# Second transform: the last three block products of a column group accumulated in one pair of banks, two column groups alternating

## The chip, the core and the metric

The kernel runs on one core of a Trainium2 chip. The metric is the device time of one execution in microseconds (us); the median of three runs before the change is 1871.7 us (1870.88 to 1874.08).

Five instruction queues work side by side: TensorE (PE; its weight loads are shown apart as PEld), VectorE (DVE), ScalarE (ACT), GpSimd (POOL) and SyncE (SP), which here issues almost all transfers. Matrix products end in eight accumulator banks of 128 x 512 fp32 (PSUM), from which VectorE or ScalarE takes them away.

## The reference

Four layers follow each other on a 2048 x 512 activation, each added to its input: Fourier mixing, segmented attention with a memory, Fourier mixing again, attention again. The change is in the third layer.

```
def _A_ref(x, dft_seq_re, dft_seq_im, dft_hid_re, dft_hid_im):
    a = jnp.einsum("bsd,ed->bse", x, dft_hid_re)
    b = jnp.einsum("bsd,ed->bse", x, dft_hid_im)
    y = jnp.einsum("ts,bse->bte", dft_seq_re, a) - jnp.einsum("ts,bse->bte", dft_seq_im, b)
    return y
...
x = x + _A_ref(_layernorm(x, axis=-1), A_dft_seq_re, A_dft_seq_im, A_dft_hid_re, A_dft_hid_im)
x = x + _B_ref(_layernorm(x, axis=-1), B_wq, B_wk, B_wv, B_wo, B_beta)
x = x + _A_ref(_layernorm(x, axis=-1), A_dft_seq_re, A_dft_seq_im, A_dft_hid_re, A_dft_hid_im)
x = x + _B_ref(_layernorm(x, axis=-1), B_wq, B_wk, B_wv, B_wo, B_beta)
```

## The kernel before

**The transforms.** The kernel swaps the two matrix products of the mixing: first over the sequence (cosine and sine matrix, 2048 x 2048 each), then over the hidden dimension. The 2048 result columns are handled in four column groups of 512 (`tcn` 0 to 3). Every fp32 operand is split into a high and a low part (`split`, lines 97 to 107: ScalarE writes the high part, VectorE the low one), and `matmul3` (lines 109 to 112) takes high x high, high x low and low x high, so that one 128 x 128 by 128 x 512 product is three matmuls.

**First and second transform.** The first (`direct`, `contract`) multiplies plainly. As it goes, it writes sums and differences of the matrix blocks to scratch memory (`sums`, line 301), and the second transform uses them in a seven-product scheme for a 2 x 2 block product in place of eight. A product (`P1` to `P7`) runs over eight steps `k`; a step is one right-hand block `t` of 128 x 512, and two left-hand column blocks `m` = 0, 1, each with its own bank and three matmuls: six matmuls a step. The left-hand sides come from `left`: normalised rows `xa` (P1, P7, P2, P4), and combinations of rows made by `add_rows`, `xb` (P6 and P5) and `xs` (P3).

**Order of the products.** `PHASES` sets it. In the first four phases two products run interleaved, step by step, for two column groups in turn. In the last phase P6, P5 and P3 run interleaved, for each of the four column groups: 24 steps a group, 96 in all, in six banks at a time. `bank` (line 117) hands out the eight banks in rotation, so a product's first matmul waits until the earlier user of that bank has been taken away.

**Taking away.** When a product is done, `product` (lines 349 to 358) adds it to or subtracts it from each block `c[tcn, j]` that has it as a term, as `TERMS` lists: in the last phase P6 goes into three blocks, P5 into two and P3 into one, each in two halves `m`. That is 12 VectorE instructions `c<-c,m` (line 358) for a column group. `c` then is read by `split_u` (tiles `us`), and by the hidden-dimension products `y` (`hidden`, `hidden_last`).

**Right-hand blocks.** `read_block` (line 258) has SP read the raw block into a ring of eight (`cring`), from the given matrix (`in_ct`) for P1, P2 and P3 and from the sums (`sum`) for the others, and then splits it into a tile `chi` or `clo`. Despite the names, each such tile holds a high and a low part; the two names alternate, with three buffers each, so that six blocks may be ready at a time.

**Order of the work.** `place` puts generators at numbered slots, and the loop at line 1058 runs through the slots. A step of a product is one slot; a block is read ten slots and split four slots ahead of it. PE keeps that order. On the other engines a scheduler may move an instruction that is ready earlier.

Of the kernel before, what the change touches and what calls it, by code (L numbers as in the profile page):

```python
# [14 lines left out]
ALU = mybir.AluOpType  # L15
# [24 lines left out]
HALF = NT // 2  # L40
# [4 lines left out]
    "P7": (((1, 1), (0, 1), ALU.add),),  # L45
    "P2": (((0, 0), (0, 1), ALU.add),),
    "P4": (((1, 0), (1, 1), ALU.add),),
    "P6": tuple((j, j, ALU.subtract) for j in ((0, 1), (1, 0), (1, 1))),
    "P5": tuple((j, j, ALU.add) for j in ((0, 1), (1, 1))),
    "P3": (((0, 1), (0, 1), ALU.add),),  # L50
}
PHASES = (
    (("P1", "P7"), (0, 1)),
    (("P2", "P4"), (0, 1)),
    (("P1", "P7"), (2, 3)),
    (("P2", "P4"), (2, 3)),
    (("P6", "P5", "P3"), range(4)),
)


# [1 line left out]
def spectral_infini_kernel(  # L62
# [13 lines left out]
    V, A, G, T = nc.vector, nc.scalar, nc.gpsimd, nc.tensor  # L76
# [6 lines left out]
    def in_order(engine, name):  # L83
        op = getattr(engine, name)

        def call(*args, **kwargs):
            return tc.keep_in_program_order(op(*args, **kwargs))  # L87

        return call

    T = SimpleNamespace(matmul=in_order(T, "matmul"), transpose=in_order(T, "transpose"))
# [5 lines left out]
    def split(hi, lo, src, scale=1.0, lo_engine=V, hi_engine=None):  # L97
        if hi_engine is V:
            return V.tensor_copy(hi, src), V.tensor_tensor(out=lo, in0=src, in1=hi.bitcast(F32), op=ALU.subtract)  # L99
        else:  # L100
            pin(A.activation(hi, src, AF.Copy, scale=scale))  # L101
        if scale == 1.0:
            lo_engine.tensor_tensor(out=lo, in0=src, in1=hi.bitcast(F32), op=ALU.subtract)  # L103
        else:
            V.scalar_tensor_tensor(
                lo, src, scale, hi.bitcast(F32), op0=ALU.mult, op1=ALU.subtract
            )

    def matmul3(ps, lhsT, rhs, first, last):
        T.matmul(ps, lhsT(0), rhs(0), start=first, stop=False)  # L110
        T.matmul(ps, lhsT(0), rhs(1), start=False, stop=False)
        T.matmul(ps, lhsT(1), rhs(0), start=False, stop=last)

    def rows(ap, i):
        return ap[i * P : (i + 1) * P, :]
# [1 line left out]
    def bank(name, shape=(P, 512), dtype=F32):  # L117
        return psum.tile(list(shape), dtype, name=name, tag="bank", bufs=8)

    def pair(name, tag, bufs, dtype=F32R):  # L120
        return sb.tile([P, 2, 512], dtype, name=name, tag=tag, bufs=bufs)

    def load_rows(src, name="xt"):
        t = sb.tile([P, 512], F32, name=name, tag="xt", bufs=4)
        nc.sync.dma_start(t, src)
        return t
# [32 lines left out]
    def normal(xt, mv, rr):  # L159
        xn = sb.tile([P, D], F32, name="xn", bufs=2)  # L160
        V.tensor_scalar(xn, xt, mv[:, 0:1], rr, op0=ALU.subtract, op1=ALU.mult)
        return xn
# [16 lines left out]
    def place(order, gen, *at):  # L179
        for t in itertools.chain(*at):  # L180
            slots.setdefault(t, []).append((order, gen))

    def run_from(t, n, step=1):
        return range(t, t + n * step, step)
# [7 lines left out]
    def place_spectral(x_in, x_out, t0, end, ln_at, direct):  # L192
        xa, xb, xs, us, wdt, c, right = ({} for _ in range(7))
        start = t0
# [25 lines left out]
        def add_rows(k):  # L220
            xt = [load_rows(x_in[i]) for i in (k, k + HALF)]
            yield
            e, o = (
                normal(xt[n], row_mv[:, i], row_r[:, i : i + 1])
                for n, i in enumerate((k, k + HALF))
            )
            a, b = slice(0, D // 2), slice(D // 2, D)
            V.tensor_tensor(out=e[:, b], in0=o[:, b], in1=e[:, b], op=ALU.subtract)
            V.tensor_tensor(out=e[:, a], in0=e[:, a], in1=e[:, b], op=ALU.add)
            V.tensor_tensor(out=o[:, a], in0=e[:, a], in1=o[:, a], op=ALU.subtract)  # L230
            xb[k] = pair("xb", "w", 16)
            split(xb[k][:, 0], xb[k][:, 1], e)
            if k % 2 == 0:
                xs[k // 2] = pair("xs", "w", 16)
            half = xs[k // 2][:, :, k % 2 * 256 : (k % 2 + 1) * 256]
            split(half[:, 0], half[:, 1], o[:, a])
            yield

        def left(name, k, h, m):
            src, col = {  # L240
                "P1": (xa.get(k), 0),
                "P7": (xa.get(k), 2),
                "P2": (xa.get(k + HALF), 0),
                "P4": (xa.get(k + HALF), 2),
                "P6": (xb.get(k), 0),
                "P5": (xb.get(k), 2),
                "P3": (xs.get(k // 2), k % 2 * 2),
            }[name]
            return src[:, h, (col + m) * P : (col + m + 1) * P]

        def new_right(src):
            tag = ("chi", "clo")[count[0] % 2]
            count[0] += 1
            t = pair(tag, tag, 3)
            split(t[:, 0], t[:, 1], src)
            return t

        def read_block(tcn, name, k):
            if not ring:
                ring.append(sb.tile([P, 2 * LT, 512], F32, name="cring", tag="xT", bufs=1))  # L260
            raw = ring[0][:, blocks_read[0] % (2 * LT)]
            blocks_read[0] += 1
            j = SOURCE[name]
            if isinstance(j, tuple):
                nc.sync.dma_start(raw, ct[j[0], tcn, k, :, j[1]])
            else:
                nc.sync.dma_start(raw, sums[tcn, k][j])
            yield
            right[tcn, name, k] = new_right(raw)
            yield  # L270
# [64 lines left out]
        def product(tcn, name):  # L335
# [22 lines left out]
                        V.tensor_tensor(out=dst, in0=c[tcn, base][:, m], in1=ps[m], op=op)  # L358
            yield

        def split_u(tcn, tt):
            sl = slice(tt * P, (tt + 1) * P)
            for cc in range(2):
                home = ("ut", 8) if (tcn, cc) == (TC - 1, 1) else ("w", 16)
                us[tcn, tt, cc] = t = pair("us", *home)
                for half in range(2):
                    hi, lo = (
                        t[:, h, half * 256 : (half + 1) * 256].rearrange("p (m s) -> p m s", s=P)
                        for h in range(2)
                    )  # L370
                    split(hi, lo, c[tcn, (half, cc)][:, :, sl])
            yield
# [45 lines left out]
        if direct:  # L418
            for tcn in range(TC):
                t = start + 8 * HALF * tcn  # L420
                place(2, contract(tcn), run_from(t, 4 * HALF, 2))
                for k in range(HALF):
                    place(3, read_pairs(tcn, k), [t + 8 * k - 12, t + 8 * k - 4, t + 8 * k + 3])
        else:
            t = start
            for names, tcns in PHASES:
                for tcn in tcns:
                    for n, name in enumerate(names):
                        at = run_from(t + n, HALF, len(names))
                        place(2, product(tcn, name), at)  # L430
                    for k in range(HALF):
                        for n, name in enumerate(names):
                            u = t + k * len(names) + n
                            place(3, read_block(tcn, name, k), [u - 10, u - 4])
                    t += HALF * len(names)
            u = t - 4 * 3 * HALF
            for k in range(HALF):
                place(3, add_rows(k), [u - 48 + 6 * k, u - 44 + 6 * k])
        for k in range(2 * DT):
            cc, d = k // DT, k % DT  # L440
            tag = "craw" if k < 2 else ("chi", "clo")[k % 2]
            t = end - 7 + k if k < 2 else end - 3 + (k - 2) // 2
            place(3.5, load_split(wdt, (cc, d), wd[cc, d], "wdt", tag, 2 if k < 2 else 3), [t - 5, t])
        nh = 2 * DT * LT
        for tcn in range(TC):
            if tcn == 0:
                at = [end + k // 2 for k in range(nh)]
            elif tcn < TC - 1:
                at = [end + nh // 2 + ((tcn - 1) * nh + k) // 3 for k in range(nh)]
            else:  # L450
                at = run_from(end + nh // 2 + 2 * nh // 3 + 1, 2 * DT, 2)
            for tt in range(LT):
                place(3.7, split_u(tcn, tt), [at[tt * 2 * DT if tcn < TC - 1 else 0] - 4])
            place(4, (hidden if tcn < TC - 1 else hidden_last)(tcn), at)
# [554 lines left out]
    def w_at(b):  # L1009
        return lambda k: b - 52 + 2 * k if k < 12 else b - 14 + 2 * (k - 12)  # L1010

    place_spectral(
        x_tiles, mids[0], a1, b1 - LEAD,
        [((0,), a1 - 36), ((HALF,), a1 - 2)] + [((k, k + HALF), a1 - 6 + 8 * k) for k in range(1, HALF)],
        True,
    )
    place_attention(mids[0], mids[1], b1, w_at(b1), lambda k: b1 + LB + 8 + k // 2)
    place_spectral(
        mids[1], mids[2], a2, b2 - LEAD,
        [((2 * j, 2 * j + 1), a2 + t) for j, t in enumerate((-40, -24, -8, 2, 14, 20, 32, 38))],  # L1020
# [83 lines left out]
```

## Time and profile before

| | |
|---|---|
| median of three runs | 1871.7 us (1870.88 to 1874.08) |
| profiled execution, time | 1868.32 us |
| profiled execution, span | 1866.6 us |
| mean granted TensorE clock | 0.989 |
| busy: PE / DVE / ACT / POOL | 95% / 70% / 57% / 28% |
| second transform: products with `xa` from, with `xb` and `xs` from, `y` from | 934.1 / 1134.4 / 1271.2 us |

The span is from the first to the last profiled instruction; 1.72 us of the profiled execution's time lie outside it. A row of a timeline gives the start, the length, the engine, the line, the tiles (written<-read), and the number of instructions that follow each other; in brackets stands how long the engine was idle before it and whose end released it. Matmuls overlap in the pipeline, so what counts is the distance between starts, not the length.

### The profile page before, as it was taken

Reading aid. Unit: us, or ns where it says so; the run is one execution under the profiler, and the core shown is the slowest. Engines: PE = TensorE matmul, PEld = TensorE weight load, DVE = VectorE, ACT = ScalarE, POOL = GpSimd, SP = SyncE. Lnnn points to the kernel's source line nnn. Section 1 sums busy time; section 2 is a strip of 40 time slices with the busy share of each in tenths; the row PEclk is TensorE's granted clock in tenths of the full one; section 3 lists DMA queues with packets and bytes.
Section 4 is the critical chain, followed back from the end, with each engine's and each line's share of the span. In section 5 each row is a group of like instructions: output and inputs, shape, how many; then the busy total and the mean of one; then the engine's idle time right before and its main releaser. Section 6 shows DMA issues by size and latency. Waiting matters only on the chain. (4 is left out here: it accounts for less than half of the span.)

```text
span 1866.6 us, 32022 instructions
## 1 busy us (share of the span) xinstructions
PE 1781.6 (95%) x10336; PEld 1291.0 (69%) x10336; DVE 1315.2 (70%) x4073; ACT 1056.1 (57%) x2292; POOL 526.1 (28%) x831
## 2 busy tenths in 40 slices
PE   7999999999889999999899999999988999999998
PEld 6788888888556666665468888778865566666555
DVE  7854544663787887877967686768557778787684
ACT  3222221432678787778864455444427877777785
POOL 4400000003345354445542000000124444444442
PEclk9999999999999999999999999999998999999999
DMA  6766556453534443435357687654544334344331
GB/s 214 225 217 214 189 181 210 161 170 127 177 125 134 131 134 104 147 119 181 106 170 231 196 259 215 180 170 141 172 144 142 121 113 150 120 132 136 121 122 51
DMA packets 165656, 296.50 MB, mean 159 GB/s; under 512 B 17776, under 2 KB 66928, under 8 KB 165488
## 3 DMA queue, kind: packets, MB, share of 16 engines
q1 hardware_dynamic: 162224, 293.68, 49.9%
q8 instruction: 81, 1.33, 0.3%
q10 hardware_dynamic: 3264, 0.79, 0.2%
q14 instruction: 87, 0.71, 0.1%
HBM read 192.95 MB, written 100.66 MB: 157 GB/s over the span
## 5 line engine op out<-in xcount | busy, mean ns | idle before, releaser
L605 DVE CUSTOM_DVE_ANT_0 junk<-nat,mask 128x512 bf16<-128x512 f32 (+3 forms) x1024 | 496.3, 485 | 196.6 <-PE nat L87 162.2
L671 ACT ACTIVATE pT<-sT 128x512 f32<-128x512 f32 x640 | 371.5, 599 | 13.5 <-ACT sT L670 1.7
L674 POOL TENSOR_SCALAR_AFFINE_SELECT pT<-pT 128x256 f32<-128x256 f32 (+1 forms) x448 | 198.6, 457 | 451.8 <-ACT pT L671 388.1
L87 PE MATMUL u<-chi,xa 128*128 128x512 f32 x1024 | 317.3, 391 | 7.3 <-DVE xa L99 7.3
L87 PE MATMUL sT<-stkq,stkk 99*128 99x256 bf16 (+3 forms) x1024 | 249.1, 306 | 10.1 <-DMA stkq<-mt 4.6
L87 PE MATMUL nat<-stkk,stkq 96*128 96x512 bf16 (+3 forms) x1024 | 247.0, 303 | 7.1 <-DVE mx L605 2.7
L670 ACT ACTIVATE sT<-sT 128x256 f32<-128x256 f32 (+1 forms) x640 | 207.3, 335 | 53.0 <-PE sT L87 48.3
L87 PEld LDWEIGHTS u<-chi,xa 128*128 128x128 f32 x1024 | 193.5, 189 | 47.2 <-ACT chi L101 7.3
L144 POOL TENSOR_TENSOR r<-ve,half_neg 128x2 f32<-128x2 f32 (+1 forms) x33 | 22.7, 688 | 665.2 <-DVE ve L142 660.1
L87 PE MATMUL u<-clo,xa 128*128 128x512 f32 x512 | 201.5, 394 | 2.4 <-DVE clo L103 2.0
L87 PE MATMUL y<-wdt,us 128*128 128x512 f32 x768 | 181.9, 390 | 0.0
L87 PEld LDWEIGHTS <-stkk 99*128 99x128 bf16 x1024 | 82.2, 99 | 136.7 <-issue 122.9
L87 PEld LDWEIGHTS y<-wdt,us 128*128 128x128 f32 x768 | 143.6, 188 | 29.7
L87 PE MATMUL pv_bank<-pT,vt 128*17 128x512 f32 (+3 forms) x2048 | 151.2, 435 | 0.0
L87 PEld LDWEIGHTS <-stkq 96*128 96x128 bf16 x1024 | 94.6, 99 | 62.4 <-issue 22.8
L87 PE MATMUL pvv<-wv,xT 128*128 128x512 f32 x384 | 129.8, 451 | 3.7 <-DVE mx L605 3.7
L87 PE MATMUL pqk<-xT,wq 128*128 128x512 f32 x384 | 130.3, 448 | 0.0
L87 PE MATMUL po<-wo,oh 128*128 128x512 f32 x384 | 122.3, 433 | 4.2 <-DVE mx L605 2.2
L87 PE MATMUL pqk<-xT,wk 128*128 128x512 f32 x384 | 124.7, 433 | 0.0
L87 PEld LDWEIGHTS u<-clo,xa 128*128 128x128 f32 x512 | 96.6, 189 | 26.6 <-DVE clo L103 6.7
L87 PEld LDWEIGHTS pv_bank<-pT,vt 128*17 128x17 f32 x2048 | 53.6, 97 | 85.9 <-issue 82.7
L101 ACT ACTIVATE chi<-cring 128x512 fp32r<-128x512 f32 x112 | 70.6, 630 | 69.3 <-DVE clo L103 35.0
(138 smaller groups left out, 3038.3 us busy)
## 6 DMA issues: line engine op xcount, KB each, us to landing
sum<-sring SPq DMA_DIRECT2D x32, 1024.0 KB
cring<-sum SPq DMA_DIRECT2D x128, 256.0 KB
stkq<-scrq SPq DMA_DIRECT2D x64, 384.0 KB
stkk<-scrk SPq DMA_DIRECT2D x64, 384.0 KB
cring<-in_ct SPq DMA_DIRECT2D x96, 256.0 KB
sring<-in_ct SPq DMA_DIRECT2D x32, 512.0 KB
xt<-mid SPq DMA_DIRECT2D x64, 256.0 KB
craw<-in_ct SPq DMA_DIRECT2D x30, 512.0 KB
```

The costliest lines, as they stand in the source:

```text
L87: return tc.keep_in_program_order(op(*args, **kwargs))
L101: pin(A.activation(hi, src, AF.Copy, scale=scale))
L144: G.tensor_tensor(out=r, in0=ve, in1=half_neg[:, :n], op=ALU.pow)
L605: V.tensor_tensor_reduce(junk[:, :n], src, mask[:, 512 - n :], 1.0, 3e38, ALU.add, ALU.min, dst,)
L670: A.activation(blocks, blocks, AF.Relu)
L671: A.activation(dst, ps, AF.Exp, scale=-SCALE)
L674: G.affine_select(blocks, blocks, pattern=[[0, n] for n in blocks.shape[1:-1]] + [[1, P]], compare_op=ALU.is_ge, fill=0.0, base=0, channel ...
```

## The change

In the last phase the three products are no longer kept apart. `product` no longer handles P6, P5 and P3; a new function `chained` opens two banks for a column group, runs the eight steps of P6 in them, adds the two banks to `c[tcn, (1, 0)]`, goes on in the same two banks with P5 without clearing them, adds P6 + P5 to `c[tcn, (1, 1)]`, goes on with P3 and adds P6 + P5 + P3 to `c[tcn, (0, 1)]`. That is six instructions `c<-c,m` for a column group in place of 12. For the sums to come out with one sign, `add_rows` makes two of its three combinations with the opposite sign, with `scalar_tensor_tensor` in place of `tensor_tensor`.

Two column groups alternate: eight steps of P6 for group 0, eight of P6 for group 1, then P5 for group 0, P5 for group 1, P3 for 0, P3 for 1; then the same for groups 2 and 3. The number of steps (96), of matmuls and of blocks read stays as it was; the reading order of the blocks follows the new order of the steps. `add_rows` stays at the same slots: its last call ends two slots ahead of the phase.

```
 CHAIN = {"P6": (1, 0), "P5": (1, 1), "P3": (0, 1)}
...
+            V.scalar_tensor_tensor(e[:, a], e[:, a], -1.0, e[:, b], op0=ALU.mult, op1=ALU.subtract)
+            V.scalar_tensor_tensor(o[:, a], e[:, a], -1.0, o[:, a], op0=ALU.mult, op1=ALU.subtract)
...
+        def chained(tcn):
+            ps = [bank(f"m{m}") for m in range(2)]
+            for name, j in CHAIN.items():
+                for k in range(HALF):
+                    t = right[tcn, name, k]
+                    for m in range(2):
+                        matmul3(
+                            ps[m],
+                            lambda h: left(name, k, h, m),
+                            lambda h: t[:, h],
+                            (name, k) == ("P6", 0),
+                            k == HALF - 1,
+                            skip_group_check=True,
+                        )
+                    if k < HALF - 1:
+                        yield
+                for m in range(2):
+                    dst = c[tcn, j][:, m]
+                    V.tensor_tensor(out=dst, in0=dst, in1=ps[m], op=ALU.add)
+                yield
...
+            u = t
+            for tcns in (0, 1), (2, 3):
+                at = {tcn: [] for tcn in tcns}
+                for name, tcn in itertools.product(CHAIN, tcns):
+                    at[tcn] += run_from(t, HALF)
+                    for k in range(HALF):
+                        place(3, read_block(tcn, name, k), [t + k - 10, t + k - 4])
+                    t += HALF
+                for tcn in tcns:
+                    place(2, chained(tcn), at[tcn])
             for k in range(HALF):
                 place(3, add_rows(k), [u - 48 + 6 * k, u - 44 + 6 * k])
```

On PE, the place where one pair of banks follows another. Before, at the end of column group 1's 24 steps and the start of group 2's (`m0` and `m1` are the two banks of a product, the numbers tell the products apart, `chi` and `clo` are right-hand blocks):

```order
L87 MATMUL m0_12676<-chi_12856,xb_12388 128x512 x3
L87 MATMUL m1_12677<-chi_12856,xb_12388 128x512 x3
L87 MATMUL m0_12688<-clo_12866,xs_12311 128x512 x3
L87 MATMUL m1_12689<-clo_12866,xs_12311 128x512 x3
L87 MATMUL m0_12922<-chi_12876,xb_11829 128x512 x3
L87 MATMUL m1_12923<-chi_12876,xb_11829 128x512 x3
L87 MATMUL m0_12934<-clo_12892,xb_11829 128x512 x3
L87 MATMUL m1_12935<-clo_12892,xb_11829 128x512 x3
L87 MATMUL m0_12946<-chi_12906,xs_11832 128x512 x3
L87 MATMUL m1_12947<-chi_12906,xs_11832 128x512 x3
```

After the change, on PE, the end of group 1's P6 and the start of group 0's P5 (banks 12406 and 12407, which group 0's P6 filled eight steps earlier):

```order
L84 MATMUL m0_12490<-chi_12518,xb_12308 128x512 x3
L84 MATMUL m1_12491<-chi_12518,xb_12308 128x512 x3
L84 MATMUL m0_12490<-clo_12528,xb_12388 128x512 x3
L84 MATMUL m1_12491<-clo_12528,xb_12388 128x512 x3
L84 MATMUL m0_12406<-chi_12538,xb_11829 128x512 x3
L84 MATMUL m1_12407<-chi_12538,xb_11829 128x512 x3
L84 MATMUL m0_12406<-clo_12548,xb_11906 128x512 x3
L84 MATMUL m1_12407<-clo_12548,xb_11906 128x512 x3
```

Where six new banks were wanted within three steps, two wanted again are those of eight steps ago.

On VectorE, the taking away of column group 0 among the splits of right-hand blocks (`cring` is the raw ring). Before, its 12 instructions stand among six splits (behind the 26th to the 32nd of the phase); the first of them:

```order
L103 TENSOR_TENSOR clo_12634<-cring_10387,clo_12634 128x512
L358 TENSOR_TENSOR c_10870<-c_10870,m0_12406 128x512
L358 TENSOR_TENSOR c_11417<-c_11417,m0_12406 128x512
L358 TENSOR_TENSOR c_10906<-c_10906,m0_12406 128x512
L103 TENSOR_TENSOR chi_12648<-cring_10387,chi_12648 128x512
L358 TENSOR_TENSOR c_10870<-c_10870,m1_12407 128x512
L358 TENSOR_TENSOR c_11417<-c_11417,m1_12407 128x512
L358 TENSOR_TENSOR c_10906<-c_10906,m1_12407 128x512
L358 TENSOR_TENSOR c_10870<-c_10870,m0_12418 128x512
L103 TENSOR_TENSOR clo_12660<-cring_10387,clo_12660 128x512
L358 TENSOR_TENSOR c_10906<-c_10906,m0_12418 128x512
```

After the change, the taking away of group 0's P6:

```order
L100 TENSOR_TENSOR clo_12486<-cring_10387,clo_12486 128x512
L376 TENSOR_TENSOR c_11417<-c_11417,m0_12406 128x512
L100 TENSOR_TENSOR chi_12498<-cring_10387,chi_12498 128x512
L376 TENSOR_TENSOR c_11417<-c_11417,m1_12407 128x512
L100 TENSOR_TENSOR clo_12508<-cring_10387,clo_12508 128x512
L100 TENSOR_TENSOR chi_12518<-cring_10387,chi_12518 128x512
L100 TENSOR_TENSOR clo_12528<-cring_10387,clo_12528 128x512
L100 TENSOR_TENSOR chi_12538<-cring_10387,chi_12538 128x512
```

Two instructions stand alone there, behind the splits of steps 12 and 13 of the phase, and such a pair comes again every eight splits (behind 12 and 13, 20 and 21, and so on to 92 and 93; the last pair behind all 96). Outside this phase the queues keep their order, but for a few neighbours that change places on VectorE, SP and GpSimd in the stretch of the `y` products and in the attention behind it; ScalarE's order is the same throughout.

More of the change, by code (lines that the diff above doesn't have):

```diff
@@ L47 @@
     "P4": (((1, 0), (1, 1), ALU.add),),
-    "P6": tuple((j, j, ALU.subtract) for j in ((0, 1), (1, 0), (1, 1))),
-    "P5": tuple((j, j, ALU.add) for j in ((0, 1), (1, 1))),
-    "P3": (((0, 1), (0, 1), ALU.add),),
 }
+CHAIN = {"P6": (1, 0), "P5": (1, 1), "P3": (0, 1)}
 PHASES = (
@@ L56 @@
     (("P2", "P4"), (2, 3)),
-    (("P6", "P5", "P3"), range(4)),
 )
@@ L107, in split, with matmul3 @@
             )
[L109 to L112, printed above, removed]
+    def matmul3(ps, lhsT, rhs, first, last, **kw):
+        T.matmul(ps, lhsT(0), rhs(0), start=first, stop=False, **kw)
+        T.matmul(ps, lhsT(0), rhs(1), start=False, stop=False, **kw)
+        T.matmul(ps, lhsT(1), rhs(0), start=False, stop=last, **kw)
     def rows(ap, i):
@@ L228, in add_rows @@
             V.tensor_tensor(out=e[:, b], in0=o[:, b], in1=e[:, b], op=ALU.subtract)
-            V.tensor_tensor(out=e[:, a], in0=e[:, a], in1=e[:, b], op=ALU.add)
-            V.tensor_tensor(out=o[:, a], in0=e[:, a], in1=o[:, a], op=ALU.subtract)
+            V.scalar_tensor_tensor(e[:, a], e[:, a], -1.0, e[:, b], op0=ALU.mult, op1=ALU.subtract)
+            V.scalar_tensor_tensor(o[:, a], e[:, a], -1.0, o[:, a], op0=ALU.mult, op1=ALU.subtract)
             xb[k] = pair("xb", "w", 16)
@@ L435, in place_spectral @@
                     t += HALF * len(names)
-            u = t - 4 * 3 * HALF
+            u = t
[8 more added lines that the diff above has]
+                    place(2, chained(tcn), at[tcn])
             for k in range(HALF):
```

## The prediction

> **What bounds the kernel now.** I read the page first, then busy times by stretch, then the waits and the timeline of the stretch that the change touches.
>
> ```profile
> span 1866.6 us, 32022 instructions
> PE 1781.6 (95%) x10336; PEld 1291.0 (69%) x10336; DVE 1315.2 (70%) x4073; ACT 1056.1 (57%) x2292; POOL 526.1 (28%) x831
> ...
> 1134.36:1271.15 136.79, 132.24 (x578) 107.64 (x576) 91.86 (x145) 62.87 (x102) 0.00 (x0) 1.00 0.60 171
> 1134.36:1168.36 34.00, 34.00 (x152) 28.15 (x151) 20.95 (x33) 15.81 (x25) 0.00 (x0) 1.00 0.65 185
> 1168.36:1173.13 4.77, 3.25 (x13) 2.09 (x12) 4.77 (x9) 1.27 (x2) 0.00 (x0) 1.00 0.48 121
> 1203.08:1207.85 4.77, 3.25 (x13) 2.10 (x12) 4.77 (x9) 1.27 (x2) 0.00 (x0) 1.00 0.43 123
> 1237.80:1242.58 4.78, 3.27 (x14) 2.10 (x12) 4.78 (x9) 1.26 (x2) 0.00 (x0) 1.00 0.44 125
> ```
>
> TensorE is busy for 95% of the span, so a microsecond counts where it takes one from TensorE. The rows with a colon are stretches: length, busy time of PE, PEld, DVE, ACT and POOL, granted clock, DMA share, GB/s. The first is the whole last phase of products: PE busy 132.24 of 136.79 us, at full clock. The second, inside it, has no idle time. The last three are short stretches around the change of column group, and there it is VectorE that is busy throughout (4.77 of 4.77) and PE that is not.
>
> ```profile
> 1134.36 1.52 PE L87 MATMUL m<-chi,xb 128*128 128x512 f32 x6
> 1135.72 1.52 PE L87 MATMUL m<-clo,xb 128*128 128x512 f32 x6
> ...
> 1168.36 1.52 PE L87 MATMUL m<-clo,xb 128*128 128x512 f32 x6
> 1170.02 0.93 PE L87 MATMUL m<-chi,xs 128*128 128x512 f32 x3
> 1172.33 0.97 PE L87 MATMUL m<-chi,xs 128*128 128x512 f32 x3 [1.38 <-DVE c L358]
> 1173.13 1.55 PE L87 MATMUL m<-clo,xb 128*128 128x512 f32 x6
> ...
> 1269.79 1.52 PE L87 MATMUL m<-clo,xs 128*128 128x512 f32 x6
> 1271.15 32.13 PE L87 MATMUL y<-wdt,us 128*128 128x512 f32 x141
> ```
>
> A step, six matmuls, takes 1.36 us from start to start (1134.36 to 1135.72), so a matmul 0.227. At the change of group P3's first step is late, and halves of it stand 2.31 us apart in place of 0.68: its banks still hold P5 of the group before. The releaser is `c` of line 358. In all of the phase PE waits for no other engine:
>
> ```profile
> PEld m L87 <- DVE c L358: 5.4, 3, 1.8
> PE m L87 <- DVE c L358: 4.1, 3, 1.4
> ```
>
> Three waits, one at each change of group; the weight load in front of a matmul waits for the same thing. The burst behind them, on VectorE at the second change:
>
> ```profile
> 1200.93 2.47 DVE L358 TENSOR_TENSOR c<-c,m 128x512 f32<-128x512 f32 x4
> 1203.32 0.68 DVE L103 TENSOR_TENSOR clo<-cring,clo 128x512 fp32r<-128x512 f32 x1
> 1203.92 0.68 DVE L358 TENSOR_TENSOR c<-c,m 128x512 f32<-128x512 f32 x1
> ```
>
> One taking away occupies VectorE for 0.60 us from start to start (1203.32 to 1203.92, the split likewise; four in 2.47 us), so 12 and the splits between them hold it for over 10 us.
>
> **The change part by part.**
>
> *Removed: the three waits.* The phase has 96 steps: 96 x 1.36 = 130.56 us. It takes 1271.15 - 1134.36 = 136.79. The excess is 6.23 us. By place: from 1168.36 to 1173.13 stand two steps, 4.77 - 2.72 = 2.05 us too long, the same at the two other changes (4.77 and 4.78), in all 6.16; the rest is some hundredths in the steps behind each. If no bank is waited for, the term is **-6.2 us**.
>
> *Added: a wait on the same two banks.* P5 of a column group may begin only when P6's two `c` instructions have read its banks, and so with P3 after P5: two handovers for each of four groups, eight new waits. In between run eight steps of the other group, 8 x 1.36 = 10.88 us. The taking away takes part of it. VectorE may split the block of step n once step n-6 is over (six tiles), and the order has the first `c` in front of the split of step 13. Counted from the end of step 7: the first `c` can start when the first half of step 8 is through, 0.68 later, plus some 0.16 until the last matmul is out (a row's length of 1.52 for six, against 1.36 of distance): 0.84. It holds up the split of step 13, which follows at 1.44; the second `c` stands at 2.04 and ends at 2.72, which is 1.36 after the end of step 8. The banks are wanted 10.88 after it. **Slack 9.5 us, cost 0.** Without that cover it would be the two instructions in full, 0.60 + 0.68 and the 0.16, so 1.4 us at each of eight handovers.
>
> *What queues behind the waiting `c`.* The splits of steps 13 and 14. Without the `c`, the split of step 13 would start some 0.63 us after step 7, behind ScalarE's part:
>
> ```profile
> L101 ACT ACTIVATE chi<-cring 128x512 fp32r<-128x512 f32 x45 | 28.5, 632 | 38.3 <-DVE clo L103 24.8 <-PE m L87 13.6
> L103 DVE TENSOR_TENSOR clo<-cring,clo 128x512 fp32r<-128x512 f32 x46 | 31.8, 692 | 21.4 <-ACT clo L101 21.0
> L358 DVE TENSOR_TENSOR c<-c,m 128x512 f32<-128x512 f32 x44 | 28.2, 682 | 2.7 <-PE m L87 2.7
> ```
>
> So it is 0.8 us late (1.44 against 0.63) and ends at 2.13; PE wants it at step 13, five steps of 1.36, 6.8 us, after the end of step 7. Slack 4.7 us. The split of step 14 is 0.65 late, that of step 15 on time. SP's read into the ring slot that a split frees is late by as much. SP's longest wait for a split is already 2.8 us, at a change of group (below, in all, times, longest), and no wait of ScalarE or VectorE for a transfer shows in the phase. Cost 0.
>
> ```profile
> SPq L267 <- DVE chi L103: 31.6, 28, 2.8
> ```
>
> *Removed: 24 taking-aways on VectorE*, 24 x 0.60 = 14.4 us of its time. Of it three bursts are the waits counted above; the fourth falls in the first `y` products, which VectorE's full stretch does not hold up:
>
> ```profile
> 1271.00:1283.00 12.00, 12.00 (x55) 9.93 (x54) 12.00 (x27) 6.18 (x18) 0.00 (x0) 1.00 0.34 95
> 1283.00:1350.00 67.00, 67.00 (x305) 55.46 (x304) 40.52 (x97) 26.15 (x65) 7.84 (x8) 1.00 0.58 174
> ```
>
> PE is busy without a break from 1271 to 1350. Worth 0 there.
>
> *Changed: 16 half-width operations in `add_rows`.* The form added is not in the trace at 128x256. The nearest are the one replaced, and the same operation at 128x512:
>
> ```profile
> L229 DVE TENSOR_TENSOR xn<-xn x8: 410/416/421, 1023.1 to 1127.7; 128x256 f32<-128x256 f32 x8
> L533 DVE SCALAR_TENSOR_TENSOR phi<-praw,phi x48: 674/703/1410, 438.8 to 1780.5; 128x512 f32<-128x512 f32 x48
> L103 DVE TENSOR_TENSOR xb<-xn,xb x8: 682/685/693, 1074.6 to 1131.8; 128x512 fp32r<-128x512 f32 x8
> ```
>
> At full width the median is 703 ns against 682 to 693 for plain operations, so at half width I take 0.42 us, as now: 0. The bounds: nothing, and the full-width maximum 1.41 for each, 16 x (1.41 - 0.42) = 15.8 us more on VectorE over some 105 us (1023 to 1128).
>
> *Moved: the rows are wanted sooner.* `xb` of the eighth row pair is read at step 8 now, not at step 22: at 1134.36 + 7 x 1.36 = 1143.9. It is there at 1131.8 + 0.69 = 1132.5: slack 11.4 us. Only at the bound of 15.8 would it be late, by 4.4. `xs` is wanted at step 33, later than before.
>
> *Moved: reads.* 96 of 256 KB on SP's queue as before, one for each 1.36 us, but 16 from one source in a row where three sources took turns. Phase and neighbour stretch move 171 to 185 GB/s at a DMA share of 0.60 to 0.65; I see no row that makes the sources differ. 0, at worst a block late at each of four changes to `in_ct` or back, a step each: 5 us.
>
> **Sum:** -6.2 against the profiled execution: span 1866.6 to 1860.4, time 1868.32 to 1862.1. That execution lies 3.4 us below the median of the runs, 1871.7; on the runs' scale the same sum gives **1865.5 us**.
>
> A rule that speaks against the change: the Trainium skill, Perfetto Trace Analysis, section Optimizing Tensor Performance, says that independent matmul groups should rotate through different banks, so that one is taken away while the next runs. By that rule the chain is the wrong way round. The trace agrees that rotation alone is not enough: rotating through eight banks with six at a time is what waits 2.05 us here. The rival "the banks are waited for" below is that rule at work.
>
> **The rivals.**
>
> *The banks are waited for (slower).* If VectorE reaches the pair of `c` only behind work that lasts beyond the other group's eight steps, each of eight handovers waits. Priced by the present late handover, 2.05 us: 16.4 - 6.2 = +10.2, so 1881.9; with the bare 1.4 us, 11.2 - 6.2 = +5.0, so 1876.7. It turns slower once a handover costs 6.2 / 8 = 0.78 us, when the pair ends 9.5 + 0.78 = 10.3 us later than I have it. For it: a late taking away is just what holds PE now. Against: two instructions among splits that need 0.60 of every 1.36 us, not 12 in a burst.
>
> *The time is lost again further on (little or no gain).* Attention follows, and PE waits there for others:
>
> ```profile
> 1400.00:1860.00 460.00, 434.45 (x3163) 276.02 (x3163) 352.83 (x1449) 355.35 (x846) 202.35 (x359) 0.99 0.38 120
> ```
>
> 25.6 us of PE's time there are idle. If those waits hung on something that does not start earlier, the 6.2 would melt into them: half of it gives 1868.6, all 1871.7. Against: all that stands there hangs on `y`, which starts earlier by the whole amount, behind nearly unchanged queues.
>
> *Rows or blocks late (gain partly given back).* At the bounds above 4.4 us at the first P6 or 5 us at the reads: -1.8 or -1.2, so 1869.9 or 1870.5. Against: slacks of 11.4 us, and of ten slots between read and use.
>
> **How the numbers follow.** What can be told from no change is 0.2%, 3.7 us: faster is below 1868.0, slower above 1875.4. Forecast 84%: its own range is the sum with 1 us of shift downstream and the spread of runs (0.8 below, 2.4 above the median): 1863 to 1869. Melting 8%, late rows or blocks 3%, banks waited for 5%. I set the range from 1862 to 1870.2: it takes in the half-lost gain and the late rows, and leaves out the slower case. Faster: the forecast but for the runs that its spread lifts over 1868.0, 0.82; same: those, and the two middle rivals, 0.13; slower 0.05.
>
> **What would show it.** Right: in the changed profile the first `xb` product and the first `y` lie 130.6 us apart in place of 136.8; no row of PE waiting for `c`; six `c<-c,m` a group, each pair starting within 3 us of its product's end; VectorE some 14 us less busy; all after `y` moved by the same 6 us. Wrong: PE waits in front of the first `xb` matmul of P5 or `xs` matmul of P3 (banks), of step 8 (`xb`), or for `chi` and `clo` released by a transfer (reads); or `y` starts 6 us earlier and the end does not move, which is the melting case.

## The result, and the profile after

| | median, us | lowest to highest | runs |
|---|---|---|---|
| before | 1870.64 | 1868.13 to 1874.08 | 6 |
| changed | 1862.48 | 1860.58 to 1865.16 | 6 |

The ratio is 0.9955, with a 95% interval from 0.9942 to 0.9968: 8.2 us less by the medians, where 6.2 were forecast. The profiled execution of the changed kernel is its slowest one, 1865.16 us, with a span of 1863.4.

The page of the changed kernel, span and busy times of the engines:

```profile
span 1863.4 us, 31984 instructions
...
PE 1782.8 (96%) x10336; PEld 1291.9 (69%) x10336; DVE 1302.3 (70%) x4049; ACT 1056.1 (57%) x2292; POOL 524.6 (28%) x831
```

The number of matmuls is unchanged, VectorE has 24 instructions fewer and 12.9 us less to do. Next the changed phase, first the stretch from the first `xb` product to the first `y` (length, then busy time of PE, PEld, DVE, ACT, POOL, granted clock, DMA share, GB/s):

```profile
1139.64:1270.20 130.56, 130.56 (x578) 108.11 (x576) 82.50 (x128) 62.87 (x102) 0.00 (x0) 1.00 0.59 182
```

130.56 us in place of 136.79, and TensorE busy through all of it. The timeline of TensorE around the first of the eight new handovers (the 16th step, the last of group 1's P6, starts at 1160.04; the row at 1161.40 is the first P5 step of group 0, in the banks of its own P6):

```profile
1157.32 1.52 PE L84 MATMUL m<-clo,xb 128*128 128x512 f32 x6
1158.68 1.52 PE L84 MATMUL m<-chi,xb 128*128 128x512 f32 x6
1160.04 1.52 PE L84 MATMUL m<-clo,xb 128*128 128x512 f32 x6
1161.40 1.52 PE L84 MATMUL m<-chi,xb 128*128 128x512 f32 x6
1162.76 1.52 PE L84 MATMUL m<-clo,xb 128*128 128x512 f32 x6
```

Each step starts 1.36 us after the one before, the handover too. On VectorE at the same place the pair of `c` of group 1's P6 stands alone among the splits:

```profile
1159.54 0.69 DVE L100 TENSOR_TENSOR clo<-cring,clo 128x512 fp32r<-128x512 f32 x1 [0.67 <-ACT clo L98]
1160.92 0.69 DVE L376 TENSOR_TENSOR c<-c,m 128x512 f32<-128x512 f32 x1 [0.68 <-PE m L84]
1161.52 0.68 DVE L100 TENSOR_TENSOR chi<-cring,chi 128x512 fp32r<-128x512 f32 x1
1162.13 0.68 DVE L376 TENSOR_TENSOR c<-c,m 128x512 f32<-128x512 f32 x1
1162.72 0.68 DVE L100 TENSOR_TENSOR clo<-cring,clo 128x512 fp32r<-128x512 f32 x1
1163.62 0.69 DVE L100 TENSOR_TENSOR chi<-cring,chi 128x512 fp32r<-128x512 f32 x1 [0.22 <-ACT chi L98]
```

It is through at 1162.81, and group 1's next product wants the banks at 1160.04 + 9 x 1.36 = 1172.28. In the view of waits of this stretch TensorE has no row at all; the longest rows with `c` or its banks are of the other engines, and cost TensorE nothing:

```profile
DVE c L376 <- PE m L84: 8.2, 12, 0.7
ACT chi L98 <- PE m L84: 8.1, 12, 0.7
ACT clo L98 <- DVE c L376: 8.0, 11, 0.7
```

What this leaves open is the rest of the gain. A table of stages, from starts in the traces and rounded to 0.1 us, shows where it can be (us; the kernels below the second line are those of the experiments):

| kernel | first `y` of layer 1 to first `m` | first `xb` to first `y` | first to last `y` | last `y` to end |
|---|---|---|---|---|
| before | 571.1 | 136.8 | 105.9 | 489.5 |
| changed | 577.7 | 130.6 | 105.9 | 487.3 |
| before, again | 574.7 | 136.8 | 105.9 | 493.1 |
| signs alone | 571.1 | 136.8 | 105.9 | 487.6 |
| changed, again | 574.5 | 130.6 | 105.9 | 485.8 |
| without alternation | 576.3, 574.7 | 137.9, 137.9 | 105.9, 105.9 | 490.5, 487.3 |
| order alone | 573.4 | 130.6 | 105.9 | 485.3 |
| one by one | 575.5, 576.0 | 130.6, 130.6 | 105.9, 105.9 | 485.3, 485.6 |
| changed, 8 instructions more | 573.3 | 131.5 | 105.9 | 487.8 |
| before, 64 instructions more | 573.7 | 139.3 | 105.9 | 485.9 |

The two product stages repeat to 0.1 us where the matmuls and the waits are the same. The attentions do not: the stretch with the first one, far ahead of the change, took between 571.1 and 577.7 us. In the profiled execution of the changed kernel it was 6.6 us longer than before the change; the `xa` products behind it took 1.5 us less, so that the phase starts 5.3 us later (1139.64 against 1134.36). A single pair of executions therefore doesn't tell what the whole is worth; the medians do.

What goes with this scatter is the granted clock, the share of full speed that TensorE gets. From the first `xb` to the last `y` it is 1.00 in every trace. In the attentions there are stretches of 3.4 us, often two in a row, in which it is 0.50, and their number and length differ between executions of one kernel. One of them, before:

```profile
479.14:485.94 6.80, 6.28 (x17) 4.10 (x18) 5.59 (x21) 0.27 (x1) 0.00 (x0) 0.50 0.96 280
```

From the last `y` of layer 1 to the first `m` the mean clock was 0.984 and 0.988 in the two shortest executions of that stretch (before and signs alone, 465.2 us each), and 0.977 to 0.978 in the three longest (changed, without alternation, one by one again: 470.1 to 471.8 us). No run varied the clock by itself, so that it is the cause is not shown.

### The profile page after: what moved, and what is told of

It reads as the page before. It is cut to its first block, busy times and chain, and to the rows that moved or that the text cites. A ratio compares the mean times of both kernels' runs of the same rounds, so it can differ in the third digit from the quotient of the medians.

```text
span 1863.4 us, 31984 instructions
## 1 busy us (share of the span) xinstructions
PE 1782.8 (96%) x10336; PEld 1291.9 (69%) x10336; DVE 1302.3 (70%) x4049; ACT 1056.1 (57%) x2292; POOL 524.6 (28%) x831
## 5 line engine op out<-in xcount | busy, mean ns | idle before, releaser
L98 ACT ACTIVATE clo<-cring 128x512 fp32r<-128x512 f32 x112 | 70.6, 630 | 62.8 <-DVE chi L100 32.0
```

## The experiments

**Do the new handovers need the second column group between them?** Everything is kept, but each group runs its P6, P5 and P3 straight through.

```
-            for tcns in (0, 1), (2, 3):
+            for tcns in (0,), (1,), (2,), (3,):
```

> The chain of the change, but the four column groups one after another, so that P5 follows P6 in the same two banks at once. Theory (banks are what counts, and the eight steps of the other group hide the taking away): eight handovers now wait. By the order on VectorE (first c, one split, second c) the second half of the next step starts some 0.8 us late; by the bare two instructions 1.4 us. So the phase from the first xb product to the first y takes 130.6 + 8 x 0.8 to 1.4 = 137 to 142 us, and the kernel is 6 to 11 us slower than the changed one, that is 1868.5 to 1873.5, about as slow as before. Rival (the gain comes from 24 fewer VectorE instructions, whatever the banks): phase 130.6 us, time as the changed kernel, 1862.5.

> The chain without alternation again: its phase is 137.9 us, 1.15 longer than before the change, and behind the phase its queues have the order of the changed kernel. Theory (only the phase counts): 1.2 us slower than before, ratio 1.0006. Rival (the order behind the phase is worth 2 us): 1 us faster than before, ratio 0.9995 or less, and the stretch from the last y to the end below 488 us in place of the 490.5 of the first look.

Measured: 1870.81 us (12 runs), ratio 0.9997 (0.9984 to 1.0009), and again 1870.63 us (12 runs), ratio 1.0004 (0.9992 to 1.0016). The gain is gone. The stretch of the phase, and TensorE's waits in it (in all, times, longest):

```profile
1138.41:1276.30 137.89, 134.97 (x578) 106.88 (x577) 82.79 (x128) 62.85 (x102) 0.00 (x0) 1.00 0.59 172
```

```profile
PE m L84 <- DVE c L376: 2.9, 16, 0.2
```

Sixteen waits, two for each of eight handovers. One of them on TensorE's timeline:

```profile
1147.93 1.52 PE L84 MATMUL m<-clo,xb 128*128 128x512 f32 x6
1149.64 0.93 PE L84 MATMUL m<-chi,xb 128*128 128x512 f32 x3 [0.19 <-DVE c L376]
1150.75 0.96 PE L84 MATMUL m<-chi,xb 128*128 128x512 f32 x3 [0.18 <-DVE c L376]
1151.55 0.63 PE L84 MATMUL m<-clo,xb 128*128 128x512 f32 x2
```

Two steps take 1151.55 - 1147.93 = 3.62 us in place of 2.72, so the handover costs 0.90; over the phase (137.89 - 130.56) / 8 = 0.92. It is less than the 1.4 that the two instructions would cost in full, because the first `c` runs while TensorE fills the second bank. The brackets show less than is lost, 0.37 of 0.90, since a row's length is that of a matmul in the pipeline. So the chain by itself, with six `c` a group, is no faster than what it replaced: eight waits of 0.92 for three of 2.05.

**Does it need the chain at all?** The kernel before, with products of their own and 12 `c` a group, but one product after the other, two groups in turn:

```
-    (("P6", "P5", "P3"), range(4)),
+    (("P6",), (0, 1)),
+    (("P5",), (0, 1)),
+    (("P3",), (0, 1)),
+    (("P6",), (2, 3)),
+    (("P5",), (2, 3)),
+    (("P3",), (2, 3)),
```

> The kernel before, with the step order of the change alone: P6, P5, P3 each as a product of its own in two banks of its own, eight steps at a stretch, two column groups alternating, and all twelve c instructions for a column group. Theory (a burst of twelve at once, with six of eight banks in use, is what held PE): the bursts are spread as 6, 4, 2 and each bank is free long before it is wanted, so the phase takes 130.6 us and the time is that of the changed kernel, 1862.5 within 2 us, though VectorE has 14 us more work. Rival (VectorE's work is what counts): the phase keeps at least half of its 6.2 us of waits, 1866 or more.

Measured: 1861.62 us (7 runs), ratio 0.9949 (0.9929 to 0.9968). The phase with the first step behind it, by stretch:

```profile
1136.43:1267.10 130.67, 130.67 (x578) 108.22 (x577) 95.18 (x152) 62.88 (x102) 0.00 (x0) 1.00 0.61 182
```

VectorE has 95.18 us to do in the phase, 12.7 more than the changed kernel, and TensorE waits as little: from the first `xb` product to the first `y` it is 130.56. Neither the smaller number of `c` nor the reuse of two banks is what pays; it is that the products run one after another. Two things come with that order, and no run parts them: fewer banks are given back at once (two, with six `c` at most, where it was six with 12), and a bank is wanted again only 24 steps after its product has ended.

**Nor the alternation of groups, then?** The same with each group's three products in a row, so that every product opens two new banks:

```
-    (("P6", "P5", "P3"), range(4)),
+    (("P6",), (0,)),
+    (("P5",), (0,)),
+    (("P3",), (0,)),
...
+    (("P3",), (3,)),
```

> As the run before, but the column groups one after another (P6, P5, P3 of group 0, then of group 1, and so on), each product in two banks of its own, twelve c instructions for a group. Theory: a bank is wanted again four products, 32 steps or 43 us, after its first use, so nothing waits: phase 130.6 us, 1862.5 within 2 us; neither the chain nor the alternation is needed when the products do not run interleaved. Rival (alternation itself is what helps): waits of about 2 us at each change of group stay, 1868.5.

> Products one after another in banks of their own, again. Theory (only the phase counts): phase 130.6 us, ratio 0.9967 within 0.0013. Rival (2 us more from the order behind the phase, which is that of the changed kernel but for one place on VectorE): 0.9955, last stretch below 488 us.

Measured: 1862.99 us (8 runs), ratio 0.9953 (0.9938 to 0.9969), and again 1863.69 us (7 runs), ratio 0.9964 (0.9949 to 0.9979); the phase is 130.56 both times. With separate banks the order of the groups doesn't matter. Alternation is needed only because the chain wants its own two banks again.

**The signs in `add_rows` alone.** The kernel before with the two `scalar_tensor_tensor` and P6 added in place of subtracted:

```
-    "P6": tuple((j, j, ALU.subtract) for j in ((0, 1), (1, 0), (1, 1))),
+    "P6": tuple((j, j, ALU.add) for j in ((0, 1), (1, 0), (1, 1))),
...
-            V.tensor_tensor(out=e[:, a], in0=e[:, a], in1=e[:, b], op=ALU.add)
-            V.tensor_tensor(out=o[:, a], in0=e[:, a], in1=o[:, a], op=ALU.subtract)
+            V.scalar_tensor_tensor(e[:, a], e[:, a], -1.0, e[:, b], op0=ALU.mult, op1=ALU.subtract)
+            V.scalar_tensor_tensor(o[:, a], e[:, a], -1.0, o[:, a], op0=ALU.mult, op1=ALU.subtract)
```

> The kernel before with the new form of the two operations in add_rows alone (P6 is then added where it was subtracted); bursts and order of the products as before. Theory: the operation takes 0.42 us in either form, the phase 136.7 us, ratio 1.000 within 0.0012. Rival (the extra gain comes from it): ratio 0.999 or less.

Measured: 1870.96 us (12 runs), ratio 0.9995 (0.9983 to 1.0008). The rows of these instructions (shortest, median, longest in ns; first and last start):

```profile
L229 DVE SCALAR_TENSOR_TENSOR xn<-xn x8: 414/418/420, 1022.0 to 1126.6; 128x256 f32<-128x256 f32 x8
L230 DVE SCALAR_TENSOR_TENSOR xn<-xn x8: 414/423/426, 1023.0 to 1127.1; 128x256 f32<-128x256 f32 x8
```

0.42 us each, as the plain operation took. This part of the change is worth nothing either way.

**How far do medians of one kernel agree?** The kernel before and the changed one were run once more, unaltered.

> The kernel before, unchanged, timed against itself: shows how far times and stage lengths differ between executions. Theory (the changed kernel's gain is the 6.2 us of the phase, and the 8.2 between the medians is that plus the spread): ratio 1.000 within 0.15%, and the stretch from the first y of the first transform to the first product of the second, and the one from the last y to the end, differ by 2 to 5 us from those of the first profile although nothing is changed. Rival (2 us of the gain come from another place by way of the change): those stretches repeat within 1 us, and the time from the last y to the end is 489.5 again against 487.3 with the change.

> The changed kernel again. Theory (the whole gain is the 6.2 us of the phase, the rest is spread): phase 130.6 us, ratio 0.9967 within 0.0013, and from the last y to the end between 485 and 493 us, as the kernel before has. Rival (some 2 us more come from behind the phase, where the scheduler let a few neighbours change places): ratio 0.9955 again, and the last stretch below 488.

Measured: before 1872.59 us (12 runs), ratio to itself 1.0002 (0.9991 to 1.0014); changed 1861.64 us (7 runs), ratio 0.9955 (0.9938 to 0.9972). Both signs of the rival came out for the changed kernel: the ratio is 0.9955 again, and the last stretch 485.8. Of the two other repetitions the one without alternation has the time of its theory (1.0004) and the last stretch of its rival (487.3); one by one has 0.9964, which is nearer its theory, and 485.6. And the kernel before, unaltered, differs from its first profile by 3.6 us in both attentions, as its theory had it.

So runs must be pooled. The 73 of the kernel before that were timed beside the changed kernel and beside these experiments have a mean of 1871.6 +- 0.7 us (95%); the 35 of the three kernels whose TensorE doesn't wait in the phase (changed, order alone, one by one) 1862.7 +- 0.9. The difference is 8.9 +- 1.2 us, of which the phase is 6.2. Some 2.7 us more are gained elsewhere, known to 1.2.

**Where the rest comes from.** Behind the last `y` TensorE's work is the same in all kernels. In the first 55 us of the second attention (from 5 to 60 us behind the last `y`) one wait separates them. Before:

```profile
PE nat L87 <- DMA stkk<-scrk: 2.3, 1, 2.3
```

The changed kernel:

```profile
PE nat L84 <- DMA stkk<-scrk: 0.8, 1, 0.8
```

The kernel before again, the signs alone and both runs without alternation have 2.5, 2.6, 2.5 and 2.5; changed again, order alone and one by one 0.9, 0.8, 0.7 and 0.7. So it goes with the late handovers, but the last of them is more than 130 us earlier. What else differs is the length of TensorE's queue: the kernels with late handovers have 213 entries in it that only wait, the others 205. And the DMA engines carry packets of 16 KB on a queue of their own, q8, 81 in the run: 10336 matmuls, as many weight loads and 213 waits are 81.6 times 256. The Trainium skill, Runtime: NRT & Kernel Launch, section Instruction fetch mechanics, says that a sequencer fetches its own instructions through its own DMA queue in blocks of 16 KiB, 256 instructions each, which the count bears out, and that the cost is mostly hidden. Whether such a packet meets the transfer `stkk<-scrk` was tried from both sides, by adding TensorE instructions to the phase. First 8 (four matmuls and their weight loads) to the changed kernel; a repeated first matmul clears its bank again and changes no value:

```
                     for m in range(2):
+                        if (name, k, m) == ("P6", 0, 0):
+                            T.matmul(ps[m], left(name, k, 0, m), t[:, 0], start=True, stop=False, skip_group_check=True)
                         matmul3(
```

> The changed kernel with four matmuls more: the first matmul of each column group's chain is issued twice (it clears its bank each time, so the result stays the same). With their weight loads these are 8 instructions more in TensorE's queue, all in the last phase. Asked is the part of the gain that lies behind the phase: kernels with the late handovers (before, and the one without alternation) have 8 waiting instructions more in TensorE's queue, and in the second attention TensorE then waits 2.3 to 2.6 us for the transfer stkk<-scrk, against 0.7 to 0.9 in the kernels without late handovers. Theory A: it is the place of TensorE's own instruction fetches (16 KB packets, one for some 256 instructions), which come 8 instructions sooner and run into that transfer. Then here the packet of the second attention comes at 135.3 to 136.9 us behind the first y product, in place of 137.1 to 137.6, and the wait is 2.3 to 2.6 us again; first xb to first y 130.6 + 4 x 0.227 = 131.5 us; in all about 1864.5 to 1866. Theory B: the late handovers themselves shift something in the queues, and the number of instructions is nothing to it. Then the wait stays at 0.7 to 0.9 us, and the whole is 0.9 us above the changed kernel, about 1863.3.

Then 64 to the kernel before:

```
                 for m in range(2):
+                    for _ in range({"P6": 2, "P5": 1, "P3": 1}.get(name, 0) if k == 0 else 0):
+                        T.matmul(ps[m], left(name, k, 0, m), t[:, 0], start=True, stop=True)
                     matmul3(
```

> The kernel before with 32 matmuls more, in the last phase: the first matmul of each bank of P6 is issued three times and that of P5 and P3 twice (each clears its bank, so the result stays the same). With their weight loads these are 64 instructions more in TensorE's queue, some 5.8 us of its stream; all three late handovers stay. Theory A (place of TensorE's instruction fetches): the packet of the second attention comes some 6 us sooner, at 130 to 131 us behind the first y product, ahead of the transfer stkk<-scrk (issued at 132 to 133), and TensorE's wait for that transfer falls from 2.3 to 2.6 us to below 1.2, although the handovers are as late as before. Theory B (the late handovers themselves): the wait stays at 2.3 to 2.6 us. By both, first xb to first y is 136.8 us and up to 32 x 0.227 = 7.3 us more (less where a repeated matmul hides in a wait); the whole 1876 to 1879.

The view of transfers, in a window from 130 to 137 us behind the first `y`, and the issue of the transfer by SP. (The instruction packets of q14 are smaller ones, of some 8 KB; one or two stand in each window, whether the wait is long or short.) The kernel before: an instruction packet of q8 falls into the window, 136.3 us behind the first `y`, 3.2 behind the issue.

```profile
q1 hardware_dynamic: 505, 0.92, 43.9%
q8 instruction: 1, 0.02, 0.9%
```

```profile
1404.31 0.47 SPq L576 DMA_DIRECT2D stkk<-scrk  x1
```

The changed kernel: none of q8; it comes at 137.1, 4.9 us behind the issue.

```profile
q1 hardware_dynamic: 834, 1.39, 61.7%
q10 hardware_dynamic: 51, 0.01, 0.8%
q14 instruction: 2, 0.02, 0.7%
```

```profile
1402.42 0.47 SPq L603 DMA_DIRECT2D stkk<-scrk  x1
```

The changed kernel with 8 instructions more: the packet comes at 136.5, 4.0 us behind the issue, and the wait is back.

```profile
q1 hardware_dynamic: 696, 1.22, 59.2%
q8 instruction: 1, 0.02, 0.9%
```

```profile
PE nat L84 <- DMA stkk<-scrk: 2.5, 1, 2.5
```

The kernel before with 64 more: the packet comes at 128.9, ahead of the window and of the issue, and the wait is gone although the handovers are late.

```profile
q1 hardware_dynamic: 646, 1.12, 52.9%
q10 hardware_dynamic: 51, 0.01, 0.8%
q14 instruction: 2, 0.02, 0.6%
```

```profile
PE nat L87 <- DMA stkk<-scrk: 0.8, 1, 0.8
```

Theory A holds in both directions, theory B falls: here the fetch is not hidden. All twelve traces agree. In the six with the long wait the packet comes 3.2 to 4.0 us behind the issue, in five with the short one 4.7 to 4.9 behind it, in the last 4.0 ahead of it. It is the transfer that is late, and not TensorE that lacks its instructions: from the issue to the matmul that waits for it pass 7.0 to 7.3 us with the long wait and 5.4 to 5.5 with the short one, and by the profile the matmul starts some 0.14 us after the landing in all of them. Before and changed:

```profile
1411.30 0.58 PE L87 MATMUL nat<-stkk,stkq 96*128 96x512 bf16 x1 [2.30 <-DMA stkk<-scrk]
```

```profile
1407.91 0.38 PE L84 MATMUL nat<-stkk,stkq 96*128 96x512 bf16 x1 [0.82 <-DMA stkk<-scrk]
```

The whole: 1866.16 us (7 runs), ratio 0.9961 (0.9933 to 0.9989), for the 8; this is 3.5 above the mean of the kernels without waits, where 0.9 for the matmuls and 1.7 for the wait are 2.6, inside the noise. For the 64: 1870.05 us (10 runs), ratio 0.9997 (0.9984 to 1.001), where both theories had 1876 to 1879; the packet came at 128.9 where theory A had 130 to 131. The phase grew by 2.5 us only (139.3), not by 7.3: most repeated matmuls fell into the late handovers (TensorE's row of waiting for `c` falls from 4.1 us to 0.5), which is what such a wait is, time in which TensorE has nothing that it may do. With 1.5 to 1.7 off for the transfer, 1 us more than before would be left; the ratio's interval goes from 3.0 us less to 1.9 more. What is lost at the wait is not won back behind it: from the last `y` to the end the changed kernel with 8 more takes 487.8 us, longer than the five executions without the long wait (485.3 to 487.3), and the kernel before with 64 more 485.9, shorter than the five with it (487.3 to 493.1). So about 1.6 of the 2.7 us have a cause that was shown.

The 1.1 us that are left are within the noise, and the granted clock of the runs takes them up. Its mean is 0.9885 over the runs of the kernel before for which it is on record (those beside the experiments and the repetition, without one of 1887.9 us at 0.936, which alone lifts the mean of the 73 by 0.2) and 0.9894 over the 35 without waits. Among runs with a clock of 0.989 the means are 1870.3 us (23 runs before) and 1863.3 (17 without waits), among those with 0.990 1869.1 (15) and 1861.1 (9): differences of 7.1 and 8.1. A straight line of time against clock, with one slope for all kernels of this document, puts the difference at 7.3 +- 0.6, where the phase and the transfer make 7.8. Why the mean clocks differ is open: both runs without alternation, which have the late handovers, have 0.9895. The long wait may have a part in it. In three of the six traces with it a stretch of half clock begins within 1.3 us of its end, in none of the six with the short wait, which is too few to call shown. Before, and the changed kernel behind the same wait:

```profile
1410.90:1414.30 3.40, 3.00 (x11) 2.07 (x12) 0.87 (x4) 0.62 (x2) 0.42 (x2) 0.50 0.03 9
```

```profile
1408.20:1411.60 3.40, 3.39 (x23) 2.23 (x22) 2.93 (x15) 2.70 (x7) 1.32 (x4) 1.00 0.07 21
```

No version tried is faster than the changed kernel by more than its runs scatter; the order alone (1861.62 us) does as well with six lines in a table.

## Why the prediction came out as it did

*The three waits, -6.2 us: right, to 0.1.* The phase takes 130.56 us in the profiled execution, the 96 x 1.36 of the sum, and as long in the four other profiled executions of kernels without these waits.

*The handover in the same two banks, cost 0: right.* By the sum the pair of `c` would start 0.84 and 2.04 us after the end of the step before its product's last and be through at 2.72. Counted from 1160.04 it starts at 0.88 and 2.09 and is through at 2.77. The split between stands at 1.48 where 1.44 was worked out. The bare price of 1.4 was an upper bound; without the cover it is 0.92.

*Splits and reads behind the waiting `c`, 0: right.* TensorE has no row of waiting for a block in the phase.

*24 taking-aways, worth 0 beyond the waits: right.* Order alone keeps them all and gains the same. VectorE's busy time fell by 12.9 us, where some 14 had been put.

*`add_rows` at 0.42 us an operation: right,* by the rows of the signs alone. `xb` and `xs` were not waited for.

*The rivals.* The banks are not waited for. Rows and blocks are not late. Melting did not happen; the deviation is on the other side. Two slips in the working changed nothing: the range to 1870.2 does not take in all of the late rows and blocks (the reads came to 1870.5), and inside the phase the source of the blocks changes three times, not four, which would have made the bound 4.1 us.

*Where it was off: the step "half of it gives 1868.6, all 1871.7" and the 1 us of shift downstream.* The prediction let what lies behind `y` give back time, and put nothing on its gaining any. Its reason was that all there "starts earlier by the whole amount, behind nearly unchanged queues". The order in the queues is nearly unchanged, but TensorE's has 8 entries fewer ahead of the second attention, and this moved an instruction fetch out of the way of a transfer that TensorE waits for. That term is -1.6 us, and with it and the rest that wasn't resolved the gain is 8.9 +- 1.2 in place of 6.2. The median of 1862.48 lies below the 1863 at which the forecast's own range ended, and inside the stated range only because that had been drawn a microsecond wider, with no term to say why: that much is luck. The mechanism of the forecast is not; its 6.2 us stand in the phase. The test that "all after `y`" moves "by the same 6 us" was a bad one: in the profiled pair the first `y` starts only 0.95 us earlier and the end 3.2, because the stages ahead of the phase had taken 5.3 us more in that execution (the first attention 6.6 more, the `xa` products 1.5 less), although TensorE's work in them is the same.

## What to carry to other kernels

Where products that run interleaved end within a few steps of each other, their banks come back in one burst, and here a rotation through eight banks did not help with six wanted at once: let the products run one after another before cutting down the number of instructions that take them away. Reusing the same banks was free with eight steps of other work (10.9 us) between, and cost 0.92 us a time with none; lengths between these were not tried. When a change gains or loses a few microseconds where it touched nothing, add some instructions that do nothing and see whether the difference moves with them, before explaining it, and compare runs at the same granted clock.

## What the runs showed that was not expected

Eight instructions on TensorE, which take less than a microsecond, made a transfer more than 130 us later hold TensorE up for 2.5 us in place of 0.8: a 16 KB packet of instructions between 3.2 and 4.0 us behind the transfer's issue made it land some 1.6 us later, one at 4.7 to 4.9 us behind it or 4.0 us ahead of it did not. That they share a DMA engine fits this but was not seen. And the stretch with the first attention, which the change does not touch, took 571.1 to 577.7 us from one execution to another, while the products from the first `xb` to the last `y` repeated to 0.1 us; by and large the longer executions are those with a lower granted clock there.
